# Dividing the last batch of an attention in two parts, and summing its features on TensorE

## The chip, the cores and the metric

The kernel runs on one core of a Trainium2 chip. The metric is the device time of one execution in microseconds (us); several executions are timed and the median counts. The profile is of one more execution. Engines are named as the profile names them: PE (TensorE's matmuls), PEld (its weight loads), DVE (VectorE), ACT (ScalarE), POOL (GpSimd), and the DMA queues that SP (SyncE) and ACT issue into, SPq and ACTq.

## The reference, cut to what matters

Sizes: 4 batches, 12 heads, 448 tokens, head size 64, so 768 features; the hidden layer has 3072.

```python
q_n, k_n = rmsnorm(q, g_q), rmsnorm(k, g_k)
scores = q_n @ k_n.T / sqrt(64);  scores -= max(scores)
attn = exp(scores);  attn = attn / (sum(attn) + 1e-9)
x = (attn @ v)                       # heads laid side by side: (batch, token, 768)
mu = mean(x); var = mean((x - mu) ** 2)
xn = (x - mu) / sqrt(var + 1e-6) * g_ln
x = x + relu(xn @ w_ch1) @ w_ch2     # first MLP
u = x + (x.T @ U @ V).T              # mix over tokens
out = u + relu(u @ w2_ch1) @ w2_ch2  # second MLP
```

The part that changes is, for the last batch only, the division by `sum(attn)` and the sum that makes `mu`.

## The kernel before, in words

**Layout.** Each batch's x lives in SBUF as `x[b]`, 128 features by 6 tiles by 448 tokens; tile k holds heads 2k and 2k+1. A matmul here has 448 moving columns. Numbers are carried as a rounded part and a remainder (`xh` and `xl` for the norm's result, `hh` and `hl` for the hidden values, two halves of each weight tile), so one product of the MLP is three matmuls. A plain float32 product appears in the trace as two records.

**Attention stage, 0 to about 370 us.** A loop over i walks the 48 heads (batch 0 to 3, 12 each), software pipelined: in step i head i has its scores made (`sc`), head i-1 its product with v (`pv`), and head i-2 its result stored (`norm`). `norm` copies the 64 rows of the undivided result and the row of the exponentials' sums out of PSUM and stores them by two DMAs on SPq, `x<-u` into `x[b]` and `sum<-u` into a DRAM tile `sum`. Each step has four slots, and in each slot the generator at the head of the list `ln` makes one step; these are the background tasks: division (`scale`), norm statistics (`ln_stats`), norm (`ln_apply`) of finished batches, and `early`, which loads and prepares the first weights. After head 35 (i = 38) the list holds `scale(2)`, `ln_stats(2)` and `early`, 12, 20 and 8 slots; the loop has 48 slots left there.

**Division (`scale`).** All 12 x 448 sums are loaded as 128 x 42 (`ss<-sum`), inverted as exp(-ln s) on ACT with a correction of three DVE instructions (L425 to L427), stored to DRAM (`rs<-sy`), and read back by two broadcast DMAs (`xl<-rs`), each to 64 partitions: 672 KB each. The tile that receives them is the one that later holds `xl`. Then six DVE multiplications (L450), one for each tile of x. For batch 3 these DMAs are in ACT's queue.

**Norm (`ln_stats`, `ln_apply`).** The sum over features: tokens 0 to 223 by two DVE reductions over the six tiles (L165), tokens 224 to 447 by five POOL additions (L167, L169); then one float32 product with a matrix of 1/768 gives the mean on every partition (`mu`, L174), ACT copies it (L177). Then for each of six tiles: x - mu (L187, on POOL and DVE in turn), square on ACT (L190), sum on DVE (L184); another product with the same matrix (`var`, L193), the inverse root (L196 to L199, L145 to L147), and in `ln_apply` for each tile: x - mu (L218), times gain and inverse root on DVE (L221), `xh` on ACT (L213), `xl` on POOL or DVE (L214). The buffers of tag `lt` (four of 128 x 448) hold mu, the running sum and the tiles in work.

**MLP stage, from about 370 us.** `mlps` walks the hidden layer in 12 chunks for each MLP. For chunk c and batch b it emits `h_unit` twice (18 matmuls each, L581) and then, for the chunk-and-batch before, `o_unit` six times (6 matmuls each, L595): e0 to e5. So the order of TensorE at the start is h of batch 0, h of batch 1, o of batch 0, h of batch 2, o of batch 1, h of batch 3, o of batch 2, in blocks of 36 matmuls. After each of these units the list `side` makes one or two steps; at the start it holds batch 3's remaining `scale`, `ln_stats` and `ln_apply`. `scale(3)`'s first six steps are made between the six tiles of `ln_apply(2)`, just before. In this order the product for `mu` comes after the first `h_unit` of batch 2, the product for `var` after o e2 of batch 1. `w_narrow` (L79 to L86) and `w_split` (L521, L522) prepare the weights of the next chunks.

**What sets the order.** An instruction in `pin(...)` stays behind the instruction that was traced just before it on its engine. All others are put in order by the framework's planner, which issues what it expects to be ready and may move an instruction far forward. Each engine then works its list in order, and an instruction that waits (a DMA that ACT issues, too) holds all behind it.

Of the kernel before, what the change touches and what calls it, by code (L numbers as in the profile page):

```python
# [3 lines left out]

# [5 lines left out]
F32 = mybir.dt.float32  # L10
# [7 lines left out]
P = 128  # L18
# [13 lines left out]
NB = 2  # L32
DL = 3
QW = D + 2
PVY = (0, 1, 2)
NL = 2
NA2 = 3
# [5 lines left out]
def f32(ap):  # L43
    return ap.bitcast(F32)


def build(tc, qkv, gg, g_ln, w1a, w2a, w1b, w2b, u_in, v_in, out):
    nc = tc.nc
    V, A, PL, PE = nc.vector, nc.scalar, nc.gpsimd, nc.tensor
    with ExitStack() as es:  # L50
# [101 lines left out]
        def ln_stats(b, pool=None):  # L152
            def lt(n, pool=None):
                if pool:
                    return pool.tile([P, S], F32, tag="lx", name=f"ln{b}_{n}", bufs=2)
                return lpool.tile([P, S], F32, tag="lt", name=f"ln{b}_{n}")

            lag = 1 if pool else 0
            xs = lt("xs")
            nv = NC // 2 if b == B - 1 else NC  # L160
            cv = slice(nv * CP, S)
            for c in range(NC):
                if c < nv:
                    cs = slice(c * CP, (c + 1) * CP)
                    V.tensor_reduce(xs[:, cs], x[b][:, :, cs].rearrange("p k n -> p n k"), AX.X, ALU.add)  # L165
                elif c == nv:
                    PL.tensor_tensor(xs[:, cv], x[b][:, 0, cv], x[b][:, 1, cv], ALU.add)  # L167
                    for k in range(2, KD):
                        PL.tensor_tensor(xs[:, cv], xs[:, cv], x[b][:, k, cv], ALU.add)  # L169
                yield  # L170
            for _ in range(4 if b == B - 1 else 1):
                yield
# [24 lines left out]
            yield  # L197
            pin(A.activation(y, a, AF.Ln))
            pin(A.activation(y, y, AF.Exp, scale=-0.5))  # L199
            yield  # L200
            rsqrt_newton(y, a, t)
            yield
            lns[b] = (mu, y)
# [18 lines left out]
                yield  # L222


        def attention(ap, ep, ep2, early):
            ggt = load_ggt(ap)
            NH = B * H
            NP = NH // 2
# [183 lines left out]
                nc.sync.dma_start(st["sum", b][h:h + 1, :], u[D:D + 1, :])  # L412
                yield

            def scale(b, q, pool=None):
                fold = "h s -> (h s)"
                s = lpool.tile([P, H * S // P], F32, tag="sc", name=f"ss{b}", bufs=2)
                q.dma_start(s, st.pop(("sum", b)).rearrange(fold).rearrange("(p n) -> p n", p=P))
                yield
                y = lpool.tile([P, H * S // P], F32, tag="sc", name=f"sy{b}", bufs=2)  # L420
# [8 lines left out]
                d = dpool.tile([H, S], F32, tag="rs", name=f"rs{b}")  # L429
                q.dma_start(d.rearrange(fold).rearrange("(p n) -> p n", p=P), y)  # L430
                yield
                rs = []
                if pool:
                    r = f32(norm_tiles(b, pool)[1])
                    for j in range(2):
                        q.dma_start(r[j * D:(j + 1) * D],
                                    d.rearrange("(k j) s -> j k s", j=2)[j:j + 1].to_broadcast([D, KD, S]))
                    rs = [r[:, hp, :] for hp in range(KD)]
                    yield
                    yield  # L440
                    yield
                for hp in range(KD + 1):
                    if hp < KD and not pool:
                        r = lpool.tile([P, S], F32, tag="lt", name=f"r{b}_{hp}")
                        for j in range(2):
                            q.dma_start(r[j * D:(j + 1) * D, :],
                                        d[2 * hp + j:2 * hp + j + 1, :].to_broadcast([D, S]))
                        rs.append(r)
                    if hp:
                        pin(V.tensor_tensor(x[b][:, hp - 1, :], x[b][:, hp - 1, :], rs[hp - 1], ALU.mult))  # L450
                        yield

            for pr in range(3):
# [6 lines left out]
            for i in range(-3 - T1, NH + 2):  # L460
# [9 lines left out]
                    ln.append(load_uv())  # L470
                if i - 2 in (H, 2 * H, 3 * H):
                    b = (i - 2) // H - 1
                    ln.append(scale(b, nc.sync, npool if b < 2 else None))
# [98 lines left out]
        def mlps(pool, start):  # L572
# [37 lines left out]
            for c in range(2 * NCH + 1):  # L610
                u = 2 * G * c
                for b in range(B):
# [32 lines left out]
                    if c == 2 * NCH:  # L645
                        break

        wpool0 = es.enter_context(tc.tile_pool(name="ring0", bufs=2))
        with tc.tile_pool(name="att", bufs=1, side="right") as ap:
            with tc.tile_pool(name="tok", bufs=1) as ep, tc.tile_pool(name="feat", bufs=1) as ep2:  # L650
                last = attention(ap, ep, ep2, early())
        xpools = [npool, npool] + [es.enter_context(tc.tile_pool(name="xn2", bufs=1, reuse_waits="tile"))]
# [3 lines left out]
        last = last(pool)  # L656
# [58 lines left out]
```

## Time and profile before

| | us |
|---|---|
| three timed executions | 1847.28, 1848.6, 1860.36 |
| median | 1848.6 |
| profiled execution, its own time | 1861.35 |
| its span in the trace | 1859.5 |
| PE busy (96% of the span) | 1792.8 |
| DVE, ACT, POOL busy | 1112.2, 565.0, 436.4 |

PE's busy time contains the waits between matmuls of a stream and the stretches at half clock, so the 96% doesn't say that only 4% can be won. The mean granted clock of the profiled execution is 0.987 of full speed.

### The profile page before, as it was taken

How to read it: one execution, taken by the hardware profiler on the slowest of the kernel's cores; microseconds unless marked ns; L12 is line 12 of the kernel's file. 1: busy time of each engine (PE TensorE's matmuls, PEld its weight loads, DVE VectorE, ACT ScalarE, POOL GpSimd, SP SyncE). 2: the span in 40 equal slices, each digit the busy share in tenths (PEclk: the TensorE clock that was granted, in tenths of full speed). 3: DMA queues.
4: the chain of work that ended last, by engine and by line, in shares of the span. 5: the costliest groups of instructions: out<-in, count | busy, mean ns of one | idle time of the engine just before them, and what ended most of it. 6: DMA issues, size and time to landing. Idle time of an engine off the chain costs nothing.

```text
span 1859.5 us, 22719 instructions
## 1 busy us (share of the span) xinstructions
PE 1792.8 (96%) x8680; PEld 1558.9 (84%) x8680; DVE 1112.2 (60%) x1941; ACT 565.0 (30%) x1145; POOL 436.4 (23%) x312
## 2 busy tenths in 40 slices
PE   5999998978999999999999999999999999999999
PEld 4666665566999999999999998999999999999998
DVE  6768787867656454555555467545555555555633
ACT  6786776522212111221212134212212122121210
POOL 5445666343201110110101123201101011010100
PEclk9999999998999999999999999999999999999999
DMA  4453434411222111212122111112111121211103
GB/s 104 106 123 74 110 73 114 104 34 52 85 68 68 35 54 49 69 39 64 36 67 69 35 35 43 43 52 69 45 59 47 56 68 37 66 43 60 35 1 119
DMA packets 72669, 116.52 MB, mean 63 GB/s; under 512 B 29744, under 2 KB 42608, under 8 KB 72560
## 3 DMA queue, kind: packets, MB, share of 16 engines
q1 hardware_dynamic: 43824, 98.50, 18.3%
q10 hardware_dynamic: 28736, 16.56, 3.7%
q8 instruction: 68, 1.11, 0.2%
q14 instruction: 41, 0.34, 0.1%
HBM read 98.35 MB, written 5.68 MB: 56 GB/s over the span
## 4 chain that ended last, share of the span: by engine, by line
PE 78%; DVE 3%; POOL 3%; issue 2%; ACT 1%; DMA 1%; ACTq 0%; POOLq 0%; DVEq 0%
PE o L595 37%; PE h L581 36%; PE po L395 1%; PE t L556 1%; POOL w L522 1%; POOL xl L214 0%; DMA xl<-rs 0%; PE ps L370 0%; DVE ln_acc L184 0%; POOL ln_d L218 0%; PE ps L371 0%; DVE m L345 0%; PE xt L547 0%; DVE x L450 0%; DVE ln_xs L165 0%
## 5 line engine op out<-in xcount | busy, mean ns | idle before, releaser
L581 PE MATMUL h<-xh,w 128*128 128x448 f32 x2304 | 662.4, 369 | 4.1 <-ACT xh L213 4.1
L595 PE MATMUL o<-hh,w 128*128 128x448 f32 x2304 | 662.3, 369 | 0.0
L581 PEld LDWEIGHTS h<-xh,w 128*128 128x128 f32 x2304 | 434.7, 189 | 44.8 <-ACT xh L213 5.1
L595 PEld LDWEIGHTS o<-hh,w 128*128 128x128 f32 x2304 | 434.1, 189 | 39.2 <-issue 0.8
L597 DVE TENSOR_TENSOR x<-x,o 128x448 f32<-128x448 f32 x576 | 350.1, 617 | 170.2 <-PE o L595 167.6
L522 POOL TENSOR_TENSOR w<-wf,w 128x768 fp32r<-128x768 f32 x96 | 184.9, 1936 | 1071.9 <-ACT w L521 1071.9
L581 PE MATMUL h<-xl,w 128*128 128x448 f32 x1152 | 423.7, 368 | 3.8 <-POOL xl L214 3.8
L595 PE MATMUL o<-hl,w 128*128 128x448 f32 x1152 | 423.3, 367 | 0.0
L585 ACT ACTIVATE hh<-h 128x448 fp32r<-128x448 f32 x192 | 103.8, 541 | 815.0 <-PE h L581 813.0
L586 DVE SCALAR_TENSOR_TENSOR hl<-h,hh 128x448 fp32r<-128x448 f32 x192 | 119.2, 621 | 330.5 <-ACT hh L585 330.3
L581 PEld LDWEIGHTS h<-xl,w 128*128 128x128 f32 x1152 | 217.3, 189 | 24.4 <-POOL xl L214 5.1
L595 PEld LDWEIGHTS o<-hl,w 128*128 128x128 f32 x1152 | 217.2, 189 | 19.5
L395 PE MATMUL po<-p,vf 112*128 112x448 f32 x384 | 180.0, 552 | 2.1 <-DVE m L345 2.1
L345 DVE TENSOR_REDUCE m<-pm 112x1 f32<-112x448 f32 x192 | 117.9, 618 | 49.4 <-PE pm L344 48.5
L80 DVE TENSOR_SCALAR wf<-wf 128x768 f32<-128x768 f32 x96 | 67.9, 707 | 127.5 <-ACT wf L79 121.1
L79 ACT ACTIVATE wf<-wr 128x384 f32<-128x384 f32 x192 | 96.6, 549 | 147.2 <-POOL w L522 146.0
L85 DVE SCALAR_TENSOR_TENSOR wf<-wr,wf 128x384 uint32<-128x384 uint32 x192 | 118.3, 637 | 1.6
L521 ACT CAST w<-wf 128x768 fp32r<-128x768 f32 x96 | 77.8, 832 | 133.0 <-DVE x L597 62.8
L86 DVE SCALAR_TENSOR_TENSOR wf<-wr,wf 128x384 uint32<-128x384 uint32 x192 | 113.1, 601 | 0.7
L374 ACT ACTIVATE p<-ps 112x448 f32<-112x448 f32 x192 | 104.3, 543 | 13.2 <-PE ps L371 12.8
L370 PE MATMUL ps<-bq,a 128*112 128x448 f32 x192 | 100.9, 526 | 1.9 <-DVE m L345 1.2
L395 PEld LDWEIGHTS po<-p,vf 112*128 112x128 f32 x384 | 75.0, 196 | 12.6 <-DVE m L345 2.5
(107 smaller groups left out, 1311.8 us busy)
## 6 DMA issues: line engine op xcount, KB each, us to landing
wr<-in_w1a SPq DMA_DIRECT2D x48, 384.0 KB
wr<-in_w2a SPq DMA_DIRECT2D x48, 384.0 KB
wr<-in_w1b SPq DMA_DIRECT2D x48, 384.0 KB
wr<-in_w2b SPq DMA_DIRECT2D x48, 384.0 KB
raw<-in_qkv ACTq DMA_DIRECT2D x42, 224.0 KB
vf<-in_qkv ACTq DMA_DIRECT2D x48, 112.0 KB
a<-a SPq DMA_DIRECT2D x48, 112.0 KB
x<-u SPq DMA_DIRECT2D x48, 112.0 KB
```

The source lines that it names most:

```text
L85: V.scalar_tensor_tensor(fu[:, n], lo, 29, fu[:, n], ALU.logical_shift_right, ALU.bitwise_or)
L86: V.scalar_tensor_tensor(fu[:, n], hi, 0x80000000, fu[:, n], ALU.bitwise_and, ALU.bitwise_or)
L345: V.tensor_reduce(m[:, c:c + 1], pm[:CP, :S], AX.X, ALU.max)
L370: PE.matmul(pb[:CP, :S], a1[:, cs], bq, start=True, stop=False)
L374: A.activation(p, pb[:CP, :S], AF.Exp)
L395: PE.matmul(po[:, :S], vf[:, j, c, :], ps[c], start=(c == 0), stop=(c == NC - 1))
L522: PL.tensor_tensor(lo, f, f32(hi), ALU.subtract)
L581: PE.matmul(ph[:, :S], wt[:, k, :], xt[:, k, :], start=(n == 0), stop=(n == 3 * KD - 1))
L585: A.activation(hh, ph[:, :S], AF.Relu)
L586: V.scalar_tensor_tensor(hl, ph[:, :S], 0.0, f32(hh), ALU.max, ALU.subtract)
L595: PE.matmul(po[:, :S], wt[:, e, :], ht, start=(n == 0), stop=(n == 3 * G - 1))
L597: V.tensor_tensor(x[b][:, e, :], x[b][:, e, :], po[:, :S], ALU.add)
```

## The change

For batch 3 alone:

- `scale` takes a range of heads. Heads 0 to 7 (`most`) are divided apart from heads 8 to 11 (`last`). `most`'s first five steps (load of sums, inverse, store) become background tasks at the end of the attention loop (slots 41 to 45 of 48); its sixth (the broadcasts, 2 x 448 KB) is made at the first step of `ln_apply(2)`, before `last`'s first.
- `last` does the same for four heads (sums 128 x 14, broadcasts 2 x 224 KB), its six steps in the same places of `ln_apply(2)` as `scale(3)`'s before, all its DMAs in ACT's queue as before. `most`'s load and store are in SP's queue, its two broadcasts in ACT's.
- In `ln_stats(3)` the two reductions and the five POOL additions go. The product with the matrix of 1/768 is made of each of the six tiles of x, added up in PSUM: six float32 products in place of one. The steps before it are three instead of eight, so with the two parts' steps `mu` now comes after o e3 of batch 0 (before: after the first `h_unit` of batch 2), `var` after o e1 of batch 1 (before: after o e2), and the DVE work of `ln_apply(3)`'s six tiles (L221) is traced before the first `w_narrow` of that chunk (before: only that of the first three).

Batches 0 to 2 keep their instructions.

```diff
-            xs = lt("xs")
-            nv = NC // 2 if b == B - 1 else NC
-            cv = slice(nv * CP, S)
-            for c in range(NC):
-                if c < nv:
+            if b < B - 1:
+                xs = lt("xs")
+                for c in range(NC):
...
+                parts = [xs]
+            else:
+                for _ in range(3):
+                    yield
+                parts = [x[b][:, k, :] for k in range(KD)]
             pm = bank("mu")
-            pin(PE.matmul(pm[:, :S], ones_m, xs, start=True, stop=True))
+            for k, t in enumerate(parts):
+                pin(PE.matmul(pm[:, :S], ones_m, t, start=(k == 0), stop=(k == len(parts) - 1)))
...
-            def scale(b, q, pool=None):
+            def scale(b, q, h0, h1, pool=None):
+
+                def fold(d):
+                    return d[h0:h1].rearrange("h s -> (h s)").rearrange("(p n) -> p n", p=P)
+
+                n = (h1 - h0) * S // P
...
-                    r = f32(norm_tiles(b, pool)[1])
+                    r = f32(norm_tiles(b, pool(), False)[1])[:, ks[0]:ks[-1] + 1, :]
                     for j in range(2):
-                        q.dma_start(r[j * D:(j + 1) * D],
-                                    d.rearrange("(k j) s -> j k s", j=2)[j:j + 1].to_broadcast([D, KD, S]))
+                        (nc.scalar if b == B - 1 else q).dma_start(r[j * D:(j + 1) * D],
+                                    d[h0:h1].rearrange("(k j) s -> j k s", j=2)[j:j + 1]
+                                    .to_broadcast([D, len(ks), S]))
...
                 if i - 2 == 3 * H:
                     ln.append(ln_stats(2, ap))
-                    ln.append(early)
+                    most = scale(B - 1, nc.sync, 0, HL, lambda: pools[-1])
+                    ln += [early, islice(most, 5)]
...
-            return lambda pool: scale(B - 1, nc.scalar, pool)
+            return most, scale(B - 1, nc.scalar, HL, H, lambda: pools[-1])
...
         for n, _ in enumerate(ln_apply(2, xpools[2])):
-            if n:
-                next(last)
-        mlps(pool, [chain(last, ln_stats(B - 1), ln_apply(B - 1, pool))])
+            next(last if n else most)
+        mlps(pool, [chain(most, last, ln_stats(B - 1), ln_apply(B - 1, pool))])
```

## Rows read from the trace of the kernel before

**Rows 1.** Windows by stage: length, busy time (records) of PE, PEld, DVE, ACT, POOL; clock, DMA.

```profile
370.36:455.07 84.71, 63.67 (x259) 54.05 (x258) 56.88 (x83) 22.60 (x43) 32.41 (x23) 0.86 0.14 37
...
396.40:404.90 8.50, 0.02 (x1) 0.01 (x1) 7.61 (x9) 0.54 (x1) 4.31 (x5) 0.80 0.00 0
...
419.60:427.00 7.40, 7.35 (x20) 5.60 (x20) 2.33 (x5) 1.12 (x2) 1.13 (x1) 0.61 0.00 0
...
430.30:440.00 9.70, 7.94 (x23) 5.87 (x24) 8.03 (x12) 1.83 (x4) 5.63 (x4) 0.65 0.00 1
```

**Rows 2.** Waits from 366 to 455 us: in total, times, longest.

```profile
PE mu L174 <- DVE ln_xs L165: 8.5, 1, 8.5
...
PE var L193 <- DVE ln_acc L184: 4.7, 1, 4.7
...
PE h L581 <- ACT xh L213: 4.1, 2, 3.3
```

**Rows 3.** Two windows of 500 us, one in each MLP; columns as in rows 1.

```profile
500.00:1000.00 500.00, 500.00 (x2421) 454.24 (x2420) 270.74 (x472) 94.75 (x170) 64.84 (x34) 1.00 0.18 54
1200.00:1700.00 500.00, 500.00 (x2468) 463.45 (x2468) 279.26 (x492) 96.51 (x173) 67.63 (x35) 1.00 0.19 56
```

**Rows 4.** Chain that ended last, 366 to 456 us: start, length, what.

```profile
383.20 0.68 DVE ln_d L221
...
386.35 1.57 DMA rs<-sy
...
388.63 8.44 DMA xl<-rs
...
397.16 4.69 DVE x L450 x6
...
402.38 2.40 DVE ln_xs L165 x2
...
404.92 1.83 PE mu L174 x2
...
419.59 1.86 PE var L193 x2
...
428.92 0.70 DVE ln_d L221
...
440.79 3.33 POOL w L522
```

**Rows 5.** Windows of 1 us within the broadcast; columns as in rows 1.

```profile
390.00:391.00 1.00, 1.00 (x7) 0.93 (x6) 0.62 (x1) 0.00 (x0) 0.00 (x0) 1.00 0.96 290
...
395.00:396.00 1.00, 1.00 (x6) 0.93 (x6) 0.00 (x0) 0.00 (x0) 0.00 (x0) 1.00 0.85 160
```

**Rows 6.** PE's timeline: start, length, instruction; a float32 product and its follower, then o.

```profile
363.46 0.92 PE L395 MATMUL po<-p,vf 112*128 112x448 f32 x2
363.86 0.71 PE L370 MATMUL ps<-bq,a 128*112 128x448 f32 x1
...
385.30 0.57 PE L595 MATMUL o<-hh,w 128*128 128x448 f32 x2
```

**Rows 7.** DVE's timeline: one L221, and the last of the norm.

```profile
442.36 2.23 DVE L221 SCALAR_TENSOR_TENSOR ln_d<-ln_d,gln,ln_acc 128x448 f32<-128x448 f32 x1
...
447.33 0.61 DVE L214 TENSOR_TENSOR xl<-ln_d,xh 128x448 fp32r<-128x448 f32 x1
```

**Rows 8.** ACT's timeline: the first copy of batch 2's norm, a relu, a square.

```profile
372.15 0.57 ACT L213 CAST xh<-ln_d 128x448 fp32r<-128x448 f32 x1 [4.40 <-DVE ln_d L221]
...
411.30 0.55 ACT L585 ACTIVATE hh<-h 128x448 fp32r<-128x448 f32 x1 [3.98 <-PE h L581]
411.74 0.57 ACT L190 ACTIVATE ln_acc<-ln_acc 128x448 f32<-128x448 f32 x1
```

**Rows 9.** SPq's timeline: the stores of the sums of heads 43 and 46.

```profile
352.40 0.43 SPq L412 DMA_DIRECT2D sum<-u  x1
...
369.07 0.43 SPq L412 DMA_DIRECT2D sum<-u  x1
```

More of the change, by code (lines that the diff above doesn't have):

```diff
@@ L1 @@
 import struct
-from itertools import chain
+from itertools import chain, islice
 from contextlib import ExitStack
@@ L34 @@
 QW = D + 2
+HL = 8
 PVY = (0, 1, 2)
@@ L158, in ln_stats @@
             lag = 1 if pool else 0
-            xs = lt("xs")
-            nv = NC // 2 if b == B - 1 else NC
-            cv = slice(nv * CP, S)
-            for c in range(NC):
-                if c < nv:
+            if b < B - 1:
+                xs = lt("xs")
+                for c in range(NC):
                     cs = slice(c * CP, (c + 1) * CP)
                     V.tensor_reduce(xs[:, cs], x[b][:, :, cs].rearrange("p k n -> p n k"), AX.X, ALU.add)
[L166 to L169, printed above, removed]
+                    yield
                 yield
-            for _ in range(4 if b == B - 1 else 1):
-                yield
+                parts = [xs]
+            else:
+                for _ in range(3):
+                    yield
+                parts = [x[b][:, k, :] for k in range(KD)]
             pm = bank("mu")
-            pin(PE.matmul(pm[:, :S], ones_m, xs, start=True, stop=True))
+            for k, t in enumerate(parts):
+                pin(PE.matmul(pm[:, :S], ones_m, t, start=(k == 0), stop=(k == len(parts) - 1)))
             yield
@@ L222, in ln_apply, with attention @@
                 yield
-        def attention(ap, ep, ep2, early):
+        def attention(ap, ep, ep2, early, pools):
             ggt = load_ggt(ap)
@@ L413, in norm @@
                 yield
-            def scale(b, q, pool=None):
-                fold = "h s -> (h s)"
-                s = lpool.tile([P, H * S // P], F32, tag="sc", name=f"ss{b}", bufs=2)
-                q.dma_start(s, st.pop(("sum", b)).rearrange(fold).rearrange("(p n) -> p n", p=P))
+            def scale(b, q, h0, h1, pool=None):
+                def fold(d):
+                    return d[h0:h1].rearrange("h s -> (h s)").rearrange("(p n) -> p n", p=P)
+                n = (h1 - h0) * S // P
+                s = lpool.tile([P, n], F32, tag="sc", name=f"ss{b}_{h0}", bufs=2)
+                q.dma_start(s, fold(st["sum", b]))
                 yield
-                y = lpool.tile([P, H * S // P], F32, tag="sc", name=f"sy{b}", bufs=2)
+                y = lpool.tile([P, n], F32, tag="sc", name=f"sy{b}_{h0}", bufs=2)
                 yield
@@ L428, in scale @@
                 yield
-                d = dpool.tile([H, S], F32, tag="rs", name=f"rs{b}")
-                q.dma_start(d.rearrange(fold).rearrange("(p n) -> p n", p=P), y)
+                d = dpool.tile([H, S], F32, tag="rs", name=f"rs{b}_{h0}")
+                q.dma_start(fold(d), y)
                 yield
-                rs = []
+                ks = range(h0 // 2, h1 // 2)
+                rs = {}
                 if pool:
-                    r = f32(norm_tiles(b, pool)[1])
+                    r = f32(norm_tiles(b, pool(), False)[1])[:, ks[0]:ks[-1] + 1, :]
                     for j in range(2):
-                        q.dma_start(r[j * D:(j + 1) * D],
-                                    d.rearrange("(k j) s -> j k s", j=2)[j:j + 1].to_broadcast([D, KD, S]))
-                    rs = [r[:, hp, :] for hp in range(KD)]
+                        (nc.scalar if b == B - 1 else q).dma_start(r[j * D:(j + 1) * D],
+                                    d[h0:h1].rearrange("(k j) s -> j k s", j=2)[j:j + 1]
+                                    .to_broadcast([D, len(ks), S]))
+                    rs = {k: r[:, k - ks[0], :] for k in ks}
                     yield
@@ L441, in scale @@
                     yield
-                for hp in range(KD + 1):
-                    if hp < KD and not pool:
-                        r = lpool.tile([P, S], F32, tag="lt", name=f"r{b}_{hp}")
+                for k in list(ks) + [ks[-1] + 1]:
+                    if k in ks and not pool:
+                        rs[k] = lpool.tile([P, S], F32, tag="lt", name=f"r{b}_{k}")
                         for j in range(2):
[L446 to L450, printed above, removed]
+                            q.dma_start(rs[k][j * D:(j + 1) * D, :],
+                                        d[2 * k + j:2 * k + j + 1, :].to_broadcast([D, S]))
+                    if k > ks[0]:
+                        pin(V.tensor_tensor(x[b][:, k - 1, :], x[b][:, k - 1, :], rs[k - 1], ALU.mult))
                         yield
@@ L472, in attention @@
                     b = (i - 2) // H - 1
-                    ln.append(scale(b, nc.sync, npool if b < 2 else None))
+                    ln.append(scale(b, nc.sync, 0, H, (lambda: npool) if b < 2 else None))
                 if i - 2 in (H, 2 * H):
@@ L646, in mlps @@
                         break
+        xpools = [npool, npool]
         wpool0 = es.enter_context(tc.tile_pool(name="ring0", bufs=2))
@@ L650, in build @@
             with tc.tile_pool(name="tok", bufs=1) as ep, tc.tile_pool(name="feat", bufs=1) as ep2:
-                last = attention(ap, ep, ep2, early())
-        xpools = [npool, npool] + [es.enter_context(tc.tile_pool(name="xn2", bufs=1, reuse_waits="tile"))]
+                most, last = attention(ap, ep, ep2, early(), xpools)
+        xpools.append(es.enter_context(tc.tile_pool(name="xn2", bufs=1, reuse_waits="tile")))
         wpool = es.enter_context(tc.tile_pool(name="ring", bufs=4, reuse_waits="tile"))
```

1 line of the change is left out of this document (removed).

## The prediction, made before the change was run

> **What bounds the kernel now.** I read the windows by stage first: outside one stretch TensorE is busy throughout the MLP at granted clock 1.00, so only the seam between attention and MLP, 370.36 to 455.07 us, can give anything here [rows 1, 3]. In it stand seven blocks of 36 MLP matmuls. The second 500 us window of the MLP has 2468 matmuls, 0.2026 us each; 252 of them are 51.1 us, and the products for mean and variance (two records each) add 0.8. So 84.7 - 51.9 = 32.8 us are lost in the seam, and that is the ceiling of any gain [rows 1, 3].
>
> Then the waits: TensorE waits 8.5 us at the mean's product, 4.7 at the variance's, 4.1 for batch 3's normed x [rows 2]. The rest of the loss is low clock after these waits: the clock averages 0.61 from 419.6 and 0.65 from 430.3, between its levels of 1.2 and 2.4 GHz [rows 1]. The chain that ended last shows what the 8.5 us hang on: a store of inverses 1.57, the broadcast 8.44 (landed at 397.07), six multiplications 4.69, the DVE reductions 2.40, the product; POOL's additions beside the reductions started after the multiplications too [rows 4].
>
> **The two paces.** In both 500 us windows the clock is 1.00 and TensorE never idle, yet one has 2421 matmuls and the other 2468: 0.2065 against 0.2026 us [rows 3]. One MLP, 12 chunks of 288 matmuls or 3456, is 13.5 us longer at the first pace. That is about the distance between the profiled execution (1861.35) or the longest timed one (1860.36) and the median 1848.6. I take it that the profiled execution ran its first MLP at 0.2065 and the median run none; what picks the pace the trace doesn't tell. The sum below is made against 1861.35, and carried over to the median by this 12.75 us.
>
> **The change, part by part.**
>
> *First eight heads.* Their sums are stored by 352.40 + 0.43 (head 43), so the load can be issued in SP's queue long before its use, if the planner moves it ahead of heads 44 to 46, whose stores queue behind it [rows 9]; head 46's store ends at 369.50, the last position it was traced behind. Two ACT instructions and three DVE ones of 128 x 28 sit in slots where the scores of attention have ended; ACT waits 4.40 us before 372.15, which covers them [rows 8]. The store of inverses goes at about 369.5 (SP), lands 1.57 later, and the broadcasts go from ACT's queue at 371.1 to 372.4. Queued behind them on ACT are batch 2's first copy (372.15 before) and the relus: 0.3 us late, or 3 late if the store falls behind head 47's stores. Nobody needs that norm before h of batch 2 at 392.6, so 3 us are hidden; without that cover they would cost 3. At zero I leave these.
>
> The broadcast of all twelve heads fills the DMA engines for six windows of 1 us (first 0.96, last 0.85), 1344 KB in 6.0 us; of its 9.1 us from first issue (387.94) to landing the other 3.1 are fixed [rows 4, 5]. Eight heads: 3.1 + 4.0, landed by about 380. Their four multiplications (0.62 to 0.78 each; 4.69 / 6 in [rows 4]) are traced behind batch 0's second relu remainder, about 381, and mix with batch 2's norm on DVE.
>
> *Last four heads.* Their steps stand where the whole division stood, behind L221 at 383.20, so the store still goes at about 386.35 and the broadcast at 387.94 [rows 4]. It lands 3.1 + 2.0 later, at 393.05, not 397.07; two multiplications end at 394.4, not 401.85. Bounds: 393.5 if DVE works the chain undisturbed, 399 if the four new multiplications delay L221 and the stores by their whole price and each meets POOL.
>
> *Sum on TensorE.* The reductions (2.40 on the chain) go. A float32 product takes 0.41 us from its start to its follower's, 363.46 to 363.86 [rows 6]: six are 2.4, in place of 0.4, so 2.0 more on TensorE. The trace shows two records to a product. By the Trainium skill, FP8 and Floating Point Precision, TensorE Precision Notes, true FP32 takes four passes; at the matmul's pace that would make 4.9 us of the 2.4 and the forecast 2.5 us later, but the spacing of the records here allows two.
>
> TensorE now comes to this product after o e3 of batch 0, 24 matmuls after 385.30, at 390.2 [rows 6]. Four of the six products run to 391.8; the fifth waits to 393.8, the sixth ends at 394.8. The wait is 2.4 us instead of 8.5 (0 to 7).
>
> *Variance.* Between mean and variance TensorE now has e4, e5, both h of batch 2 and e0, e1 of batch 1: 60 matmuls, 12.2 us, where it had 36. The chain before took from 404.92 + 1.83 to 419.59, 12.8 us, since the squares are pinned behind relus: the first square (411.74) starts right behind the relu that waited 3.98 us for h [rows 4, 8]. After the change squares 1 and 2 are still pinned behind the first relu of batch 2 and 3 and 4 behind the second. The second h ends 9.8 us after the mean, the last four steps take about 4.5, so the variance is ready at 14.3 and TensorE waits 2 us (0.5 to 4) in place of 4.7. So variance starts at 394.8 + 14.3 = 409.1, with 1 us of low clock about 410.
>
> *Batch 3's norm.* From variance to the first L221 it took 9.3 us (419.59 to 428.92), part of it an instruction pinned behind o e3's addition [rows 4]; now that stands behind e1's, already done, and I take 6: 416. From there to the last remainder at 447.94 it took 19.0 us, with weight preparation of the next chunk between: POOL's 3.33 and the DVE instructions around L221 [rows 4, 7]. These now stand behind all six L221, and batch 2's norm, the nearest case, took 372.15 to 387, about 15, with its own intrusions [rows 8]. I take 12 (10 to 16): ready at 428. After that TensorE needed 7.1 us before (447.94 to 455.07), with o of batch 2 filling the gaps before it; I take 7.5. Chunk 1 starts at 435.5 and not at 455.07.
>
> **Sum.** 455.1 - 435.5 = 19.6 us; it passes unchanged to the end, since from there TensorE is the bound. The weights for chunk 1, prepared later now, need 2 x 3.2 us of DVE and about 3 more for the last split, ready at about 437; its second h needs them at 439: nothing, or 2 us if DVE is late. Profiled execution: 1861.35 - 19.6 = 1841.8. Median: 1848.6 - 19.6 = 1829. Bounds of the terms: gain 11 (mean's wait 7, norm 16, weights late) to 26 (no waits at mean and variance, less low clock).
>
> **The rivals.**
>
> *DVE and POOL in each other's way.* The four new multiplications run while POOL works batch 2's norm. L221 at 442.36 took 2.23 us (its neighbours about 0.68) while POOL's w ran from 440.79 to 444.12 [rows 4, 7]. If each of four multiplications and two L221 lose 1.5 us that way, the last broadcast leaves up to 8 us late, TensorE waits as long as before, and the gain is what the variance and norm bring, 9 us: 1840. By the Trainium skill, SBUF — State Buffer, SBUF: two separate sides, a DVE instruction with two SBUF inputs and a POOL one that reads SBUF exclude each other for a whole instruction; the trace agrees in this pair. Against: POOL idles about a third of 372 to 386, and most multiplications of [rows 4] took 0.6 to 0.8.
>
> *The other pace.* If the first MLP falls to the pace of 0.2065, the gain stands but 12.75 come back: 1842. For: two of four executions seen. Against: the median run had not.
>
> *Low clock through the seam, the other side.* In place of one long wait come several short ones, at 391, 407, 414 and in h of batch 3. If after the first TensorE stays at 1.2 GHz to the end of the seam, about 190 matmuls cost some 0.18 more (20 records in 7.35 us from 419.6, at clock 0.61, are 0.37 each), 35 us, and the products 3; 5 of these I have counted, so 19.6 - 33 = -13: 1862. It decides from about 100 matmuls in a row at the low clock; in the trace the clock is back within each stretch (0.86 over the seam) [rows 1].
>
> *It doesn't do what it says:* if the load of the first part waits for all stores of the sums (the tile tracked as a whole), both parts travel together and only the TensorE sum and the reordering are left: 6 us at the mean, 12 in all: 1837.
>
> **How the numbers follow.** Forecast (gain 15 to 25 at 0.2026, 1824 to 1834) 0.47; other pace 0.22; DVE and POOL 0.14; parts together 0.08; more than 25 gained 0.05; low clock 0.04. A measurement of this kernel tells about 1% from no change, 18.5 us, and the forecast lies just at it: about six tenths of its case and the large gain are faster by over 1%, together with some runs compared at equal pace 0.42; slower by over 1% is half of the low clock and what I don't see, 0.04. Leaving out half of the last two cases and the tail of the other pace, the range is 1820 to 1846.
>
> **What would show it.** Right: no reduction and POOL addition of batch 3; a broadcast of eight heads landed by 382 and one of four by 394; TensorE's wait at the mean under 4 us, at the variance under 3; chunk 1 from about 436. Wrong: multiplications over 1 us each, a broadcast issued after 390, or a window of the seam with a clock under 0.7 for more than 20 us; in a profile whose seam is shorter and whose total is not, the count of matmuls in 500 to 1000 us tells the pace.

## The result, and the profile after

The changed kernel takes 1834.56 us (median of 20 runs, 1831.20 to 1849.77), the kernel before beside it 1849.86 (20 runs, 1845.62 to 1863.37). The ratio is 0.9919, 95% interval [0.9896, 0.9942]: 15 us or 0.8% faster. The forecast was 1829 and the range 1820 to 1846, so the time lies in the range and the forecast is 5.6 us too low.

The profiled execution of after takes 1834.36 us (span 1832.6) against 1861.35 (span 1859.5) before. These 27 us are not all the change's, as the windows show ("the seam" is the stretch that [rows 1] begin with): first the seam of after, from the first h of batch 0 to the first h of chunk 1, two stretches in it, and a window of 500 us in each MLP (columns as in [rows 1]).

```profile
368.80:440.20 71.40, 62.65 (x268) 52.83 (x267) 48.90 (x76) 20.64 (x40) 25.52 (x17) 0.93 0.13 33
410.00:417.00 7.00, 5.89 (x14) 4.58 (x15) 2.42 (x4) 1.52 (x3) 1.13 (x1) 0.51 0.00 0
423.00:428.00 5.00, 4.74 (x16) 4.26 (x17) 3.29 (x5) 1.14 (x2) 3.45 (x4) 0.66 0.00 2
500.00:1000.00 500.00, 500.00 (x2469) 463.48 (x2468) 278.74 (x485) 95.33 (x171) 64.11 (x34) 1.00 0.19 57
1250.00:1750.00 500.00, 500.00 (x2469) 463.47 (x2468) 277.43 (x479) 94.78 (x170) 63.69 (x34) 1.00 0.17 51
```

The seam fell from 84.7 us [rows 1] to 71.4, a gain of 13.3, at a mean clock of 0.93 and no longer 0.86. The 84.7 go by the chain that ended last; in the timeline the first h of chunk 1 starts 0.17 us sooner, so what is said below of a seam against the one before is up to 0.2 us too long:

```profile
454.90 0.57 PE L581 MATMUL h<-xh,w 128*128 128x448 f32 x2
```

The first MLP now has 2469 matmuls in 500 us where it had 2421 [rows 3]; that is the other pace. What follows the seam is 12.1 us shorter by it, and that is no work of the change. The remaining 1.6 us are an attention that ended earlier (368.80, not 370.36). The change adds only a few small steps to attention, and among the executions below its end varies from 365.5 to 374.7, so I count none of it for the change.

TensorE's waits from 366 to 442 us, to be held against [rows 2]:

```profile
PE var L193 <- DVE ln_acc L184: 4.0, 1, 4.0
PE h L587 <- ACT xh L213: 1.9, 1, 1.9
PE h L587 <- POOL xl L214: 1.8, 2, 1.0
PE o L601 <- POOL w L528: 1.1, 1, 1.1
```

The mean's wait of 8.5 us is gone altogether. The variance's stayed at 4.0, and a wait is there that was forecast nowhere: for a weight split on POOL. Where that comes from the chain that ended last shows (366 to 442 us; start, length, what), beside [rows 4]:

```profile
370.52 5.53 DMA sum<-u
...
378.72 1.85 POOL w L528
...
383.53 2.22 POOL w L528
...
385.79 4.32 PE o L601 x20
390.11 3.01 PE mu L174 x8
393.12 2.47 PE o L601 x12
...
395.80 1.57 PE mu L174 x4
...
411.11 1.86 PE var L193 x2
412.97 6.74 PE o L601 x24
...
420.27 0.69 DVE ln_d L221
```

It is read from the top. The store of head 47's sums, one row of 448 numbers, took 5.53 us from issue to landing; until then ACT's queue stood at the load of those sums (L422); the weight split, batch 2's copies and the last part came after it. Further down, TensorE runs o between two groups of mean products: the planner has put matmuls that are not pinned ahead of the products of the last tiles. Then come var, 24 matmuls of o, and the norm's first L221 behind them.

ACT's timeline from 370 to 390 us shows the hold as idle time in front of the second copy (the bracket: idle before, released by), and when the last part's store and broadcast went out:

```profile
370.94 0.57 ACT L213 CAST xh<-ln_d 128x448 fp32r<-128x448 f32 x1 [4.28 <-DVE ln_d L221]
376.07 0.36 ACTq L422 DMA_DIRECT2D ss<-sum  x1
376.48 0.57 ACT L213 CAST xh<-ln_d 128x448 fp32r<-128x448 f32 x1 [4.98 <-DMA sum<-u]
...
388.54 0.35 ACTq L434 DMA_DIRECT2D rs<-sy  x1
...
389.99 1.24 ACTq L441 DMA_DIRECT2D xl<-rs  x2
```

The DMA engines were busy throughout in that time (a share of 0.87 to 1.08 in each us from 371 to 375); the broadcast of eight heads had been issued at 369.57 (a window of 1 us, last columns DMA share and GB/s):

```profile
373.00:374.00 1.00, 1.00 (x6) 0.93 (x6) 0.00 (x0) 0.00 (x0) 0.96 (x1) 1.00 1.05 326
```

### The profile page after: what moved, and what is told of

It reads as the page before. It is cut to its first block, busy times and chain, and to the rows that moved or that the text cites. A ratio compares the mean times of both kernels' runs of the same rounds, so it can differ in the third digit from the quotient of the medians.

```text
span 1832.6 us, 22734 instructions
## 1 busy us (share of the span) xinstructions
PE 1779.2 (97%) x8690; PEld 1558.0 (85%) x8690; DVE 1111.0 (61%) x1942; ACT 565.8 (31%) x1147; POOL 429.6 (23%) x307
## 4 chain that ended last, share of the span: by engine, by line
PE 79%; DVE 3%; POOL 3%; issue 2%; ACT 1%; DMA 0%; SPq 0%; ACTq 0%; POOLq 0%; DVEq 0%
PE o L601 38%; PE h L587 37%; PE po L395 1%; PE t L562 1%; POOL xl L214 1%; DVE ln_acc L184 0%; POOL w L528 0%; POOL ln_d L218 0%; DVE m L345 0%; PE ps L370 0%; PE xt L553 0%; PE ps L371 0%; PE mu L174 0%; DMA sum<-u 0%; PE pm L344 0%
```

## The experiments

Eleven kernels ran. Each is read by its seam, measured as above (before 84.7, after 71.4 us), because medians of this kernel can't part two kernels that are 3 us apart: the interval of after's own ratio is over 8 us wide. A seam is that of one profiled execution, so a difference of 1 us between two of them counts only where the trace shows which wait it comes from.

**Each half alone.** The first kernel keeps the two parts and makes the mean as before (DVE and POOL sums, one product, at its old place in the order).

```diff
-            if b < B - 1:
-                xs = lt("xs")
...
+            xs = lt("xs")
+            nv = NC // 2 if b == B - 1 else NC
...
-                pin(PE.matmul(pm[:, :S], ones_m, t, start=(k == 0), stop=(k == len(parts) - 1)))
+            pin(PE.matmul(pm[:, :S], ones_m, xs, start=True, stop=True))
```

> The division in two parts alone: the mean's sum is made by DVE and POOL as before, and its product stands at its place of before (behind the first h of batch 2). If the two parts only bring the last tiles earlier: the last multiplication ends near 396, the reductions and POOL's additions add about 5, so TensorE waits some 5 us at the mean in place of 8.5 and 4 to 5 at the variance as before; seam (first h of batch 0 to first h of chunk 1) about 81 us against 84.7 before and 71.4 after, total 3 to 4 us under the kernel before. Rival, the division is what brings the gain: seam 74 or less, total 11 us or more under before.

The seam is 81.4 us, 3.3 less than before; the median 1844.17, ratio 0.9967 [0.9934, 1.0000]. The mean's wait is 3.5 us in place of 8.5, and the store of head 47's sums takes 5.98 us here too. The second kernel is before with the six products at the product's old place (eight empty steps ahead), undivided.

```diff
-            for _ in range(4 if b == B - 1 else 1):
...
+                for _ in range(8):
...
-            pin(PE.matmul(pm[:, :S], ones_m, xs, start=True, stop=True))
+            for k, t in enumerate(parts):
+                pin(PE.matmul(pm[:, :S], ones_m, t, start=(k == 0), stop=(k == len(parts) - 1)))
```

> The sum on TensorE alone: one division of twelve heads as before, the six products at the place of the one product of before. If the sum brings only the reductions' time: multiplications end near 402, the last product follows at once, the wait at the mean falls from 8.5 to about 6, TensorE pays 2 us for five more products; seam 82 to 84. Rival, TensorE's sum is what brings the gain, since it starts without DVE and POOL and the planner can put other matmuls between its products: seam 76 or less.

Seam 80.3 us, 4.4 less than before and less than the 82 to 84 expected; median 1847.61, ratio 0.9965 [0.9931, 0.9999]. Its waits:

```profile
PE var L192 <- DVE ln_acc L183: 4.7, 1, 4.7
PE h L580 <- POOL xl L213: 4.3, 2, 3.3
PE h L580 <- ACT xh L212: 4.2, 2, 3.6
PE mu L173 <- DVE x L449: 1.2, 1, 1.2
```

The wait at the mean is 7.3 us shorter than in [rows 2] (some 2.5 were expected): the first product starts at 397.24, right behind the first multiplication, and does not wait for the last. But the products take half of that back on TensorE (twelve records in 4.78 us; their price is worked out below). The variance's wait and that for the normed x are as in [rows 2]: neither half alone changes what follows the mean, and from the first L221 to the last remainder both kernels take 19.0 us, as before.

**The place in TensorE's order.** With both halves but the product at its old place (six empty steps, not three):

```diff
-                for _ in range(3):
+                for _ in range(6):
```

> The changed kernel with six empty steps in place of three, so that the mean's products stand where the one product stood before (behind the first h of batch 2); the parts of the division and TensorE's sum stay. Split alone took 3.2 us off the seam, the sum alone 4.3, the whole change 13.2. If the place in TensorE's order makes the rest: seam 75 to 78. Rival, the two parts help each other and the place is worth nothing: seam 71 to 73.

Seam 77.7 us, 6.3 more than after; median 1841.73, ratio 0.9950 [0.9925, 0.9975]. Its longest waits:

```profile
PE var L193 <- DVE ln_acc L184: 4.8, 1, 4.8
PE h L587 <- ACT xh L213: 4.4, 2, 3.9
```

So of the 13.3 us, 7.0 are the two halves together, and 6.3 come only once the product is also moved ahead in TensorE's order, which the change's title doesn't name: here the norm again takes 19.1 us from its first L221 to its last remainder, as before, with a weight split of POOL between (434.44, 3.34 us), and 13.8 in after. What the place alone would give without the halves was not run.

**The hold on ACT.** The hold can be taken away at either end. In one kernel the last part's load and store of sums go in SP's queue:

```diff
-            return most, scale(B - 1, nc.scalar, HL, H, lambda: pools[-1])
+            return most, scale(B - 1, nc.sync, HL, H, lambda: pools[-1])
```

> The changed kernel with the load and store of the last four heads' sums in SP's queue, so that ACT doesn't wait for head 47's sums to land (5.0 us in the changed kernel). If ACT's wait sets the pace of batch 2's norm and so of the last division: copies 4 us earlier, no wait of TensorE for the second weight split (1.1 us), last broadcast 1 to 3 us earlier, seam 69 to 70.5 against 71.4. Rival, the wait is hidden by what follows: seam 71 to 72, total within noise of the changed kernel.

Seam 69.3 us, 2.1 less than after; median 1832.91, ratio 0.9903 [0.9875, 0.9932]. ACT isn't held, both copies run at once, but the small store is still late: the load that waits for it on SP follows 5.64 us after.

```profile
372.37 0.48 SPq L412 DMA_DIRECT2D sum<-u  x1
378.01 0.34 SPq L422 DMA_DIRECT2D ss<-sum  x1
```

```profile
372.79 1.03 ACT L213 CAST xh<-ln_d 128x448 fp32r<-128x448 f32 x2 [4.29 <-DVE ln_d L221]
```

In the other the load of the last sums stands ahead of the first broadcast:

```diff
-            next(last if n else most)
+            if n == 1:
+                next(most)
+            else:
+                next(last)
```

> The changed kernel with the order of two steps exchanged: ACT issues the load of the last four heads' sums ahead of the broadcasts of the first eight. If the broadcasts (896 KB) hold up the small store of head 47's sums, the store is seen landed about 1.7 us after its issue, as in the kernel before, not 5.5, ACT waits under 2 us, and the seam is 0.5 to 3 us shorter than 71.4. Rival, the store lands late for another reason: it takes about 5.5 us here too, and the broadcasts leave after it, so the seam is longer than 71.4.

Seam 69.3 us as well; median 1833.73, ratio 0.9906 [0.9871, 0.9941]. Now nothing flows beside the store, and the load follows 1.69 us after it (the store is a row of SP's queue, the load one of ACT's):

```profile
368.70 0.43 SPq L412 DMA_DIRECT2D sum<-u  x1
```

```profile
370.39 0.36 ACTq L422 DMA_DIRECT2D ss<-sum  x1
```

The same store takes 1.7 us with the broadcast behind it and 5.5 to 6.2 beside it (five kernels with 896 KB in it). In both kernels the weight wait of 1.1 us falls to 0.2 or less, and the variance's stays at 4.0 and 4.1.

Of the 2.1 us only 1.0 is there when the variance starts (41.3 us into the seam, 42.3 in after). The other 1.1 comes behind it, where TensorE ran less long at 1.2 GHz. The 7 us from the variance's start, in after and then with the load first (clock 0.59 and 0.76):

```profile
411.11:418.11 7.00, 7.00 (x19) 5.60 (x20) 2.59 (x5) 1.12 (x2) 1.13 (x1) 0.59 0.00 0
```

```profile
408.29:415.29 7.00, 7.00 (x25) 5.83 (x26) 3.61 (x7) 1.12 (x2) 1.13 (x1) 0.76 0.00 0
```

With the last part on SP the clock is 0.76 there too. But so it is, at 0.79, in the kernel below with ten heads first, which has the longest hold. So the hold is shown to be worth about 1 us; that the rest is its work is not shown.

**How the hold grows with the broadcast.** One execution each with four heads first (448 KB in the first broadcast) and with ten (1120 KB); after has eight (896 KB).

```diff
-HL = 8
+HL = 4
```

> The changed kernel with four heads in the first part and eight in the second: first broadcasts 448 KB, second 896 KB. If head 47's small store waits for the broadcast's bytes: landed some 3.5 us after issue in place of 5.5, the second broadcast takes 2 us more to land, seam 70.5 to 73. Rival, the delay doesn't go with size: landed after 5 to 6 us.

```diff
-HL = 8
+HL = 10
```

> Ten heads first and two last, so the first broadcast carries 1120 KB while head 47's sums are stored. If the small store waits for the transfers ahead of it, its landing grows with their size: it lands 6.3 to 7 us after its issue (5.5 to 6.0 with 896 KB, 4.1 with 448 KB). Rival, the store waits only for a fixed number of descriptors ahead of it: 5 to 5.7 us again. The last broadcast is smaller, but it wasn't what ended last; the seam stays at 70 to 72 us.

With four the load follows the store by 4.07 us (367.19 to 371.26), with ten it is 6.71:

```profile
370.06 6.71 DMA sum<-u
```

So 1.7, 4.1, 5.5 to 6.2 and 6.7 us with 0, 448, 896 and 1120 KB: the delay goes by what is on its way, not by a fixed count. The seams are 72.1 and 70.0 us against 71.4: with four heads first the larger last broadcast leaves a wait of 1.6 us at the mean, and with ten the hold is longer but the low clock behind the variance shorter, as said above. In these two executions no cut of the twelve heads is shown to be the better.

**Is it the data or the place that starts the variance?** In one kernel the load stands first and the last part's steps are also made earlier, at the third tile of batch 2's norm:

```diff
-            next(last if n else most)
+            if n == 1:
+                next(most)
+            if n in (0, 1, 3, 4):
+                next(last)
+            elif n == 2:
+                next(last)
+                next(last)
```

> As with the load sent first, and the last four heads' inverse, store and broadcast traced two to three tiles of batch 2's norm earlier (correction and inverse both at the third tile, store at the fourth, broadcast at the fifth). If only that traced place holds the last broadcast back: issued near 381 in place of 387, landed by 387, the mean's products end 4 us earlier, the wait at the variance (4.1) falls under 1.5, seam 64 to 67 against 69.3. Rival, the transfers or ACT's waits for them set the time: ACT now holds batch 2's copies, the last broadcast leaves after 385, seam 69 or more.

Seam 69.7 us; median 1834.35, ratio 0.9924 [0.9893, 0.9955]. The six products run in one go, so all tiles were ready, and the variance's wait is 4.0 all the same, as the rival had it. The store of inverses went out at 379.48, but the broadcast only at 385.46, behind a relu on ACT that waits for h (TensorE's timeline, then ACT's):

```profile
390.74 4.67 PE L174 MATMUL mu<-x,ones_m 128*128 128x448 f32 x12
394.90 0.91 PE L601 MATMUL o<-hh,w 128*128 128x448 f32 x2
395.66 0.37 PE L601 MATMUL o<-hl,w 128*128 128x448 f32 x1
```

```profile
385.37 0.55 ACT L591 ACTIVATE hh<-h 128x448 fp32r<-128x448 f32 x1 [3.11 <-PE h L587]
385.46 0.58 ACTq L441 DMA_DIRECT2D xl<-rs  x1
```

In the other nothing is made ready sooner, but the mean's product and all steps behind it stand two steps earlier:

```diff
-                for _ in range(3):
+                for _ in range(1):
```

> The changed kernel with two empty steps fewer ahead of the mean's products, so that they, the squares and the variance stand two steps earlier (products behind o e1 of batch 0, variance behind o e0 of batch 1). If the chain from mean to variance is long because squares are pinned behind batch 2's relus: it falls from 14.3 us to 10 or 11, the wait at the variance from 4.0 to under 2, seam 69 to 70.5. Rival, buffers and the arrival of the last tiles set it: chain 13 us or more, and with six matmuls less ahead of the variance the wait grows to 5, seam 72 to 73.

Seam 66.1 us, 5.3 less than after; median 1832.51, ratio 0.9888 [0.9855, 0.9920]. So in after it is the place that decides. ACT's timeline of after shows how: a square stands right behind a relu that waited 2.24 us for h.

```profile
404.64 0.55 ACT L591 ACTIVATE hh<-h 128x448 fp32r<-128x448 f32 x1 [2.24 <-PE h L587]
405.08 0.57 ACT L190 ACTIVATE ln_sq<-ln_sq 128x448 f32<-128x448 f32 x1
```

Two steps earlier the chain from mean to variance falls from 13.7 to 10.9 us, as expected, and the variance waits 2.55 us, no longer 4.0 (under 2 expected). But the seam is shorter than the 69 to 70.5 expected, and that is TensorE's clock: it stays at 1.00 here. The 7 us from the variance's start, to be held against the two above:

```profile
407.34:414.34 7.00, 7.00 (x32) 5.93 (x32) 5.23 (x9) 1.12 (x2) 1.14 (x1) 1.00 0.00 0
```

So var's two records and the 24 matmuls of o behind it take 1.02 and 4.88 us in place of 1.86 and 6.74, which is 2.7 of the 5.3 us. TensorE's next waits are for chunk 1's weights (TensorE's timeline, parts of 407 to 439 us):

```profile
407.34 1.02 PE L193 MATMUL var<-ln_acc,ones_m 128*128 128x448 f32 x2 [2.55 <-DVE ln_acc L184]
...
433.85 0.47 PE L587 MATMUL h<-xh,w 128*128 128x448 f32 x1 [0.27 <-POOL w L528]
...
438.45 0.47 PE L587 MATMUL h<-xh,w 128*128 128x448 f32 x1 [0.69 <-POOL w L528]
```

These cost part of the gain: from the seam's end to the end of the program this kernel takes 1394.8 us, after 1392.4. The first 10 us of chunk 1 show it, first in this kernel, then in after (43 matmuls against 51):

```profile
433.20:443.20 10.00, 9.05 (x43) 7.74 (x43) 9.93 (x18) 4.63 (x8) 2.43 (x2) 1.00 0.39 124
```

```profile
440.20:450.20 10.00, 10.00 (x51) 9.26 (x50) 9.90 (x17) 4.20 (x8) 4.09 (x2) 1.00 0.48 160
```

**Put together.** Load first and two steps sooner:

```diff
-                for _ in range(3):
+                for _ in range(1):
...
-            next(last if n else most)
+            if n == 1:
+                next(most)
+            else:
+                next(last)
```

> The load of the last sums issued ahead of the first broadcast, and the mean's product two steps sooner. If the two gains (2 us and 5 us of the seam) are of different waits, they add: seam about 64.5 us, median some 1.5 us under the better of the two alone. Rival: in the run with the product sooner, the weights of chunk 1 already ended last, so nothing but these is left, and the seam stays at 66 us or over.

Seam 64.9 us, the shortest of all; median 1831.60, ratio 0.9917 [0.9889, 0.9946]. That is 6.5 us less than after, of the 7.4 that the two gains add up to: the clock is 1.00 behind the variance here too, so what is left of the load's place is the 1.2 us by which mean and variance both come sooner than with the product alone. From the mean's end to the variance it is 10.9 us in both, so at this place of the product earlier data do count. The profiled execution took 1846.34 us all the same, and the window says why: it has the slow pace in the first MLP.

```profile
500.00:1000.00 500.00, 500.00 (x2421) 454.17 (x2420) 270.56 (x476) 94.88 (x170) 65.25 (x34) 1.00 0.18 54
```

Then the load first, the last part's steps earlier, its store and its broadcast on SP where no relu stands ahead of them, and the product two steps sooner:

```diff
...
-                q.dma_start(fold(d), y)
+                (nc.sync if b == B - 1 else q).dma_start(fold(d), y)
...
-                        (nc.scalar if b == B - 1 else q).dma_start(r[j * D:(j + 1) * D],
+                        ((nc.sync if h0 else nc.scalar) if b == B - 1 else q).dma_start(r[j * D:(j + 1) * D],
...
```

> Load first, the last four heads' division two steps earlier, and their store and broadcast in SP's queue, where no relu holds the issue; the product two steps sooner. Theory: the last broadcast is issued by about 381.5 and not 385.5 to 388, the last two multiplications end by 390, all mean products run without a wait, the variance's wait falls under 2.5 us, and the seam is 62 to 64 us. Rival: the weights of chunk 1 (POOL's and ACT's splits, ready about 433.5) bound the seam's end, whatever the norm does: 66 us, with the waits moved to h behind those splits.

Seam 65.7 us; median 1829.36 of four runs (1827.98 to 1837.14), ratio 0.9899 [0.9883, 0.9916]. The broadcast goes out 11.3 us after the seam's start (386.00, with a seam that began at 374.72) and not 21.2, and the variance's wait falls to 2.0, both as the theory had it; but the seam isn't shorter than 64.9, and chunk 1 begins as in the kernel above, with 9.05 us busy of the first 10 and waits of 0.25 and 0.70 us behind POOL's weight splits. The theory had the mechanism of the broadcast right and its worth wrong, and one reason is again the clock. The mean ends 24.4 us into the seam and the variance starts at 38.2 (28.1 and 39.0 in the kernel above), but then the clock falls, as it doesn't there, and the first L221 comes at 46.2 and not 45.4. The 7 us from the variance's start:

```profile
412.90:419.90 7.00, 7.00 (x25) 5.70 (x26) 3.63 (x7) 1.12 (x2) 1.13 (x1) 0.76 0.00 0
```

The wait just before was 2.0 us here and 2.5 in the two kernels whose clock stayed up, so the length of this wait alone doesn't settle it; what does is open. The rival had the seam's length about right, but not the reason: the waits for chunk 1's weights stand behind the seam's end, in chunk 1 itself.

## Why the prediction was right, and where its sum was off

The seam as the only stretch to gain in, the long wait at the mean, and an order in which the wait moves on were read rightly. The sum gave 19.6 us, the seam 13.3: less than the 15 to 25 of the forecast's own case, whose times end at 1834, so that the measured time lies in the range by its width and not by the sum. Where the 6.3 us went, by the prediction's own milestones in us from the seam's start (before: [rows 4], less 370.36; for the mean's end the end of its last record):

```
                        before  forecast  after  load first  both late  two sooner
mean's product ends      36.4     24.4     28.6     27.7        32.5       29.3
variance starts          49.2     38.7     42.3     41.3        44.7       40.2
norm's first L221        58.6     45.6     51.5     49.4        53.3       46.6
norm's last remainder    77.6     57.6     65.3     63.2        72.4       58.9
chunk 1                  84.7     65.1     71.4     69.3        77.7       66.1
```

*First eight heads at zero: failed.* Load, store and broadcast went out as planned, the broadcast at 369.57. What I left out is that ACT's queue then holds the load of the last four heads' sums, which waits for head 47's store, and that this store shares the DMA engines with the broadcast that the change itself had just put there. By the Trainium skill, DMA: Bandwidth & Descriptors, Queues, rings and completion order, a store's signal lands only after every earlier write of its DMA engine, whatever the queue; that the delay grows with the bytes on their way (1.7 us with none to 6.7 with 1120 KB) agrees, though no run here parts this from a plain sharing of the engines. I priced a hold of 3 us on ACT as covered, because nobody needs batch 2's norm so soon; it was 5.0 us, and the uncovered ones behind it were the weight split (TensorE waits 1.1 us) and the last part. Without the hold the seam is 2.1 us shorter, by either way of removing it, of which 1.0 stands before the variance and the rest is low clock, as said above.

*Last four heads: 394.4 expected, 24.0 us into the seam; measured 396.1, 27.3 into it.* About 1 us of the 3.3 is the hold (with the load first the same broadcast leaves 20.3 us into the seam instead of 21.2). The rest, some 2.3, goes with DVE, within the bound that I gave (399): in after's timeline of DVE one L221 and one of the small steps of the division stand beside POOL work.

```profile
383.97 2.25 DVE L221 SCALAR_TENSOR_TENSOR ln_d<-ln_d,gln,ln_acc 128x448 f32<-128x448 f32 x1
...
387.38 1.12 DVE L431 SCALAR_TENSOR_TENSOR sy<-sy,ss 128x14 f32<-128x14 f32 x1
```

The first took 2.25 us while POOL's w ran from 383.53 to 385.74, the second 1.12, for 14 columns, while POOL's xl ran from 386.90 to 388.47; the neighbours of their kind take 0.67 and 0.16. That is the rival of DVE and POOL, at 2.5 us for these two instead of the 8 it needed to decide the time. By the Trainium skill, SBUF — State Buffer, SBUF: two separate sides, such a pair excludes each other for a whole instruction; both rows agree.

*The sum on TensorE: 2.0 us expected, 3.8 measured.* I took 0.41 us for a float32 product, from its start to its follower's. But a follower's start is no end of the product: in the timeline of the kernel with the last part early, the first o behind the products starts early in the records and the o after it late. Steady o stand 0.207 apart, so the third one at 395.66 puts the end of the products at 395.25 and six of them at 4.5 us, 0.75 each; they were 0.75 in place of one before and are 3.8 more now. The same stretched follower was there to be read in [rows 6] (363.86, 0.71 us long). By the Trainium skill, FP8 and Floating Point Precision, TensorE Precision Notes, it is four passes; at the matmul's pace I had estimated 4.9 us from it and taken the row against it. The 4.5 us measured are near it, and twice what I read from the row. On the norm's path it counts for less: the last product ends 1.3 us behind the last multiplication, where I had 0.4.

*The mean's wait: 2.4 expected, none measured.* I had TensorE wait for the last part after 24 matmuls of o. The planner instead put more of o, and one h, between the first eight records and the last four. That is no gain of its own: the matmuls that filled this gap were the ones that I had standing between mean and variance.

*The variance's wait: 2 expected (0.5 to 4), 4.0 measured.* The chain from mean to variance is right, 13.7 us against the 14.3 that I took; the work beside it is wrong, 9.7 us (397.4 to 407.1) where I counted 60 matmuls or 12.2, by the step before. And that chain isn't a chain of data: with the mean ready 2.5 us sooner (25.2 us into the seam with the last part early, 27.7 with the load first) the variance starts no sooner (41.6 and 41.3), and with all steps two places earlier it does (40.2), although that mean ends latest of the three. The squares pinned behind relus, which I had named, are what these runs and the two rows of ACT above agree with; that pin was not taken away by itself.

*Variance to the first L221: 6 expected, 9.2 measured.* I argued that the addition in front is already done. The chain shows it isn't: var, 24 matmuls of o (6.74 us), an addition, L221. But that cost little: in the kernel with the product two steps sooner the same steps stand between, and the distance is 6.5 us. What I had too small is the low clock. I had 1 us of it, and it took 2.7: var 1.86 us and the 24 matmuls 6.74, where the other kernel, at clock 1.00, has 1.02 and 4.88.

*The norm: 12 expected (10 to 16), 13.8 measured; then 7.5 expected, 6.1 measured.* The weight preparation did go behind the norm, as I had it; that it depends on the place and not on the two halves is shown by the kernel with both halves at the old place, 19.1.

*Weights of chunk 1: nothing, or 2 us.* Nothing in after. In the kernels with the product two steps sooner they are the next bound: 2.4 and 2.6 us of the gain are given back behind the seam in the two profiled at after's pace (1394.8 and 1395.0 less 1392.4).

*The two paces.* The carry-over of 12.75 us held to within 1 us (12.1 between the two profiles, behind the seam): after, at the fast pace, took 1834.36 us in the profile and 1834.56 in the median. Of the twelve profiled executions besides before's, three have the slow pace (206.67 ns from matmul to matmul, as before's has), and their rest after the seam is 1404.3 to 1405.9 us; the nine others have 202.67 ns and 1392.1 to 1395.0. The rival with this name didn't come true in the median, and what picks the pace stays open. *Low clock* came in two short stretches, as the windows above show, and not through the seam, but the first of them is the 2.7 us above.

Faster by over 1% had the chance 0.42, slower by over 1% 0.04, which leaves 0.54 for within 1%; 0.8% is at this edge, by the 6.3 us that the sum was too large.

## What to carry to other kernels

Before a transfer is made earlier, look for the small transfers that fall under it and for the queue that waits for them: a store of one row that lands 4 us late holds a whole engine if its load is issued there. When a wait at one step is removed, ask whether the next step starts by its data or by its place in the order; here moving one product ahead brought nearly as much (6.3 us) as the two halves of the change together (7.0), and at that place data 2.5 us earlier still were worth nothing. When a seam gets shorter, read the granted clock behind its waits before the gain is put down to the edit: here 1 to 3 us of it were the clock. Judge such changes by the length of the stretch that they act on, with the pace of the stretches beside it read separately.

## What the runs showed of the hardware that I had not expected

A store of one row of sums in one queue took 1.7 us alone and 4.1, 5.5 to 6.2 and 6.7 us beside a broadcast of 448, 896 and 1120 KB in another queue. A float32 product of 448 columns takes 0.75 us of TensorE, where the start of its follower in the trace suggests 0.41. The same matmuls of 448 columns, at granted clock 1.00 and with TensorE never idle, run at 202.67 or at 206.67 ns each. Behind the seam the first MLP had one of these paces to its end, every second MLP 202.67. But the pace isn't the execution's: in after it is 0.2027 us up to the mean's products, 0.2067 from there to the variance's (42 matmuls in 8.68 us, the two rows), and 0.2027 again in the MLP. In all thirteen traces, from the start of the seam to the end of the first MLP, it changes only across a float32 product or a wait of TensorE, though not across each of these.

```profile
397.62 0.57 PE L587 MATMUL h<-xh,w 128*128 128x448 f32 x2
...
406.30 0.57 PE L601 MATMUL o<-hh,w 128*128 128x448 f32 x2
```

Behind TensorE's wait at the variance the granted clock of the next 7 us was 1.00 in both kernels with a wait of 2.5 us, 0.76 in the one with 2.0, and 0.59 to 0.79 in the six with 4.0 or 4.1; in all of these 24 matmuls of o come behind it. From the variance to the first L221 that made 6.5, 8.1, and 7.9 to 9.2 us.
